# A gated feed-forward kernel on one core: the engines' programs written into the main block, without `nc.Block`

## The chip, the cores and the metric

The kernel runs on one core of one Trainium2 chip. The metric is the device time of one execution in microseconds. Every execution also has a *span*, from the first to the last recorded instruction of the kernel's own program. The time is a little longer than the span (272.68 against 270.87 us in the profiled run of the kernel before). Every profiled run has its span in the trace to the nanosecond; of all other executions the span is recorded to 0.1 us only, so a single "time minus span" of theirs can be off by 0.05 us. Landings and last records are read from the trace's records, which are finer than the views printed here.

## The reference

```python
# B, S, D, F = 32, 32, 1024, 3584; all bfloat16
def reference(x, w_gate, w_up, w_down):
    return (gelu_tanh(x @ w_gate) * (x @ w_up)) @ w_down
```

## The kernel before

The kernel records all operations of all five engines in a list, works out the semaphore waits between them, and then emits each engine's list. It is already tuned: a Strassen-like scheme saves products, and TensorE is busy nearly all the time.

The emission, in which SyncE alone waits at the end for the output transfers:

```python
    def emit(self, e, eng, sems, final=()):
        known = {}
        for op in self.ops[e]:
            ...                                    # waits that are not yet known to be met
            ins = name(eng, *args, **kw) if callable(name) else getattr(eng, name)(*args, **kw)
            if op.wanted:
                ins.then_inc(sems[op.sem], op.step)
        for name, value in final:
            eng.wait_ge(sems[name], value)
```

The block that the emission stands in. Each engine branches into a body of its own and out of it, and all meet at a barrier at the block's end:

```python
        sems, totals = pr.finish(nc, es)
        with nc.Block() as block:
            for name, e in (("sync", "sp"), ("scalar", "act"), ("gpsimd", "pool"), ("tensor", "pe"), ("vector", "dve")):
                getattr(block, name)(lambda eng, e=e: pr.emit(
                    e, eng, sems, [("out", totals["out"])] if e == "sp" else ()))
```

And the head, eight warm-up matmuls on a constant, eight transposes of the first input, then real matmuls as their weights land:

```python
        one = nc.const_aps.tensor(1.0, [P, 512], BF16)
        ...
        for n in [512] * 6 + [P] * 2:
            mm(3, one[:, 0:P], one[:, 0:n], True, True)
        for i, eng in enumerate(("sp", "act")):
            dma(eng, xn[:, 2 * i:2 * i + 2, :], x_r[:, 2 * i:2 * i + 2, 0:NX * P], 0, f"xn{i}")
        ...                                        # weights: q = 0 and 1, on SyncE and ScalarE
        for k in range(NX):
            for i, b in enumerate((6, 7) if k == 0 else (4, 5)):
                half = ps[:, b, 0:P].bitcast(BF16)
                for t in range(2):
                    pr.add("pe", "transpose", half[:, t * P:(t + 1) * P], xn[:, 2 * i + t, k * P:(k + 1) * P], ident[:, :])
                pr.add("dve", "tensor_copy", xT[0][:, k, i * 256:(i + 1) * 256], half)
```

Of the kernel before, what the change touches and what calls it, by code (L numbers as in the profile page):

```python
# [123 lines left out]
def bass_standalone__geglu_ffn__sampling_kernel(  # L124
# [19 lines left out]
    pr = _Program()  # L144

    with ExitStack() as es:
# [469 lines left out]
            dma("sp", out_r[:, 3, c0:c1], o11[:, 3, c0:c1], end, "out")  # L616

        sems, totals = pr.finish(nc, es)
        with nc.Block() as block:
            for name, e in (("sync", "sp"), ("scalar", "act"), ("gpsimd", "pool"), ("tensor", "pe"), ("vector", "dve")):  # L620
                getattr(block, name)(lambda eng, e=e: pr.emit(
                    e, eng, sems, [("out", totals["out"])] if e == "sp" else ()))


# [1 line left out]
_INS = ['x', 'w_gate', 'w_up', 'w_down']  # L626
_OUTS = [((32, 32, 1024), 'bfloat16')]
# [23 lines left out]
```

## Time and profile before

| | before |
|---|---|
| time, median of the first 3 runs | 272.45 us (272.02 to 272.67) |
| profiled run: time, span | 272.68 us, 270.87 us |
| TensorE busy | 267.8 us, 99% of the span |
| first matmul starts | 0.77 us |
| last output landed / last record | 270.459 / 270.867 us |

The profile's page of the kernel before, its head, its busy table and two of its rows by slice (each digit is the busy share, or the granted TensorE clock, of one fortieth of the span, in tenths):

```profile
span 270.9 us, 3344 instructions
PE 267.8 (99%) x1206; PEld 192.5 (71%) x1206; DVE 208.1 (77%) x246; ACT 136.1 (50%) x221; POOL 37.1 (14%) x23
PE   8999999999999999999999999999999999999996
PEclk9999999999999999999999999999999999999999
```

TensorE bounds the kernel; what a change of the program's frame can win lies in the first slice, the last one, and outside the span.

The chain of waits that ended last, in order of time (start, duration, what):

```profile
0.73 0.04 issue
0.77 3.79 PE ps L117 x16
4.56 0.05 issue
4.61 264.07 PE ps L117 x1190
268.67 0.03 issue
268.70 0.29 DVE o L117
```

The row of 1190 matmuls: all real products, 264.07 us without a gap. After it come one copy and the last output's transfer.

Seven of the eleven rows of the block's end in the kernel before (engine's queue, operation, count, duration in ns, first and last start in us; L619 is the `with` line):

```profile
L619 POOLq EVENT_SEMAPHORE  x2: 17/17/17, 270.7 to 270.8; - x2
L619 POOLq DRAIN  x1: 4349/4349/4349, 157.8 to 157.8; - x1
L619 ACTq DRAIN  x1: 519/519/519, 267.9 to 267.9; - x1
L619 DVEq DRAIN  x1: 330/330/330, 268.7 to 268.7; - x1
L619 SPq COMPARE_BRANCH  x1: 37/37/37, 270.5 to 270.5; - x1
L619 SPq DRAIN  x1: 13/13/13, 270.6 to 270.6; - x1
L619 PEldq EVENT_SEMAPHORE  x1: 51/51/51, 270.8 to 270.8; - x1
```

The drains of the other engines end by 269.04 us, while SyncE still waits for the outputs (the last landed at 270.459). Only what starts at 270.5 or later is on the path: SyncE's branch, its drain, GpSimd's two semaphore steps (gather, release) and the engines' last steps. Note that no entry branch, and no exit branch but SyncE's (37 ns), has a record.

### The profile page before, as it was taken

To read this page: it belongs to the slowest core of one execution; us is meant where nothing else is said; L and a number is where in the kernel's file an instruction comes from. 1 tells how busy PE (TensorE), PEld (TensorE's weight loads), DVE (VectorE), ACT (ScalarE), POOL (GpSimd) and SP (SyncE) were. 2 spreads that over 40 slices of the span, in tenths; PEclk is the share of its full clock that TensorE was granted. 3 is DMA by queue.
4 is the path that set the end of the run, shared out by engine and by line. 5 is a ranking of instruction groups with operands and counts; after the bars stand their busy time and mean duration, and the time that the engine had idled before them with its cause. 6 is when DMAs were issued, how large, how long until landed. Compare 5 with 4: busy or idle time off the path is not lost.

```text
span 270.9 us, 3344 instructions
## 1 busy us (share of the span) xinstructions
PE 267.8 (99%) x1206; PEld 192.5 (71%) x1206; DVE 208.1 (77%) x246; ACT 136.1 (50%) x221; POOL 37.1 (14%) x23
## 2 busy tenths in 40 slices
PE   8999999999999999999999999999999999999996
PEld 4444448888888888888776776664458888888884
DVE  1338998998899889988764839289966999999911
ACT  1339876666756675667455564521220305067452
POOL 1000003113311331134345060000000000000000
PEclk9999999999999999999999999999999999999999
DMA  7999850140491002882900070293010000002102
GB/s 211 230 333 224 243 157 4 32 123 0 130 291 46 0 0 80 239 266 73 240 0 0 0 265 8 86 348 112 0 39 19 4 0 0 0 0 80 58 21 97
DMA packets 45024, 27.47 MB, mean 101 GB/s; under 512 B 8656, under 2 KB 45008, under 8 KB 45008
## 3 DMA queue, kind: packets, MB, share of 16 engines
q1 hardware_dynamic: 42496, 25.04, 32.9%
q10 hardware_dynamic: 2512, 2.23, 3.3%
q8 instruction: 9, 0.15, 0.3%
q14 instruction: 7, 0.06, 0.1%
HBM read 23.33 MB, written 2.10 MB: 94 GB/s over the span
## 4 chain that ended last, share of the span: by engine, by line
PE 99%; DVE 0%; issue 0%
PE ps L117 99%; DVE o L117 0%
## 5 line engine op out<-in xcount | busy, mean ns | idle before, releaser
L117 PE MATMUL ps<-S,T 128*128 128x512 f32 x560 | 129.2, 392 | 0.0
L117 PEld LDWEIGHTS ps<-S,T 128*128 128x128 f32 x560 | 105.2, 188 | 22.3
L117 ACT ACTIVATE tmp<-ps 128x512 f32<-128x512 f32 x64 | 38.0, 595 | 51.7 <-PE ps L117 51.5
L117 POOL TENSOR_TENSOR T<-arena 128x1024 fp32r<-128x1024 bf16 x17 | 36.4, 2153 | 124.2 <-PE ps L117 81.8
L117 PE MATMUL ps<-T,S 128*128 128x512 f32 x224 | 51.3, 390 | 0.0
L117 DVE TENSOR_TENSOR T<-arena,T 128x1024 fp32r<-128x1024 bf16 x42 | 51.0, 1220 | 0.2
L117 PEld LDWEIGHTS ps<-T,S 128*128 128x128 f32 x224 | 42.1, 188 | 8.8
L117 ACT ACTIVATE ps<-ps 128x512 f32<-128x512 f32 x44 | 25.6, 584 | 37.0 <-PE ps L117 37.0
L117 DVE TENSOR_TENSOR hT<-tmp,ps 128x512 bf16<-128x512 f32 x56 | 36.9, 684 | 8.7 <-PE ps L117 6.7
L117 PE MATMUL ps<-arena 128*128 128x512 bf16 x192 | 43.2, 384 | 0.0
L117 DVE TENSOR_TENSOR tmp<-ps,tmp 128x512 f32<-128x512 f32 x28 | 19.4, 692 | 23.6 <-PE ps L117 23.6
L117 PEld LDWEIGHTS ps<-arena 128*128 128x128 bf16 x192 | 18.4, 99 | 23.4 <-issue 1.8
L117 DVE TENSOR_TENSOR T<-arena 128x1024 fp32r<-128x1024 bf16 x25 | 30.0, 1221 | 4.3 <-PE ps L117 4.3
L117 DVE TENSOR_TENSOR ps<-ps,tmp 128x512 f32<-128x512 f32 x32 | 22.3, 695 | 3.0 <-PE ps L117 3.0
L117 PE MATMUL ps<-arena,hT 128*128 128x512 bf16 (+2 forms) x126 | 24.6, 356 | 0.0
L117 PEld LDWEIGHTS ps<-arena,hT 128*128 128x128 bf16 x126 | 11.6, 98 | 12.8 <-issue 0.5
L117 ACT ACTIVATE tmp<-tmp 128x512 f32<-128x512 f32 x28 | 17.6, 631 | 2.4 <-DVE tmp L117 2.1
L117 ACT ACTIVATE ps<-hT 128x512 f32<-128x512 f32 x22 | 13.0, 599 | 7.6 <-DVE hT L117 7.6
L117 DVE TENSOR_TENSOR S<-hT 128x1024 fp32r<-128x1024 bf16 x14 | 16.6, 1221 | 0.0
L117 ACT ACTIVATE T<-arena 128x1024 fp32r<-128x1024 bf16 x14 | 14.8, 1060 | 0.0
L117 PE MATMUL ps<-S 128*128 128x512 f32 x56 | 12.9, 389 | 0.0
L117 ACT ACTIVATE hT<-ps 128x512 f32<-128x512 f32 x18 | 9.5, 602 | 6.1 <-PE ps L117 6.0
(33 smaller groups left out, 94.3 us busy)
## 6 DMA issues: line engine op xcount, KB each, us to landing
arena<-in_w_down_dram SPq DMA_DIRECT2D x4, 1792.0 KB, 9.7
arena<-in_w_gate_dram SPq DMA_DIRECT2D x10, 512.0 KB, 5.2
arena<-in_w_up_dram SPq DMA_DIRECT2D x10, 512.0 KB, 6.0
out_dram<-arena SPq DMA_DIRECT2D x12, 128.0 KB, 1.7
arena<-in_w_up_dram ACTq DMA_DIRECT2D x6, 128.0 KB, 4.6
arena<-in_w_gate_dram SPq DMA_DIRECT2D x3, 256.0 KB, 5.3
arena<-in_w_up_dram SPq DMA_DIRECT2D x3, 256.0 KB, 5.5
arena<-in_w_gate_dram SPq DMA_DIRECT2D x4, 128.0 KB, 3.9
```

The costliest lines, as they stand in the source:

```text
L117: ins = name(eng, *args, **kw) if callable(name) else getattr(eng, name)(*args, **kw)
```

## The change

It is meant to take away the branches into and out of the bodies and the barrier of all engines at the end. Nothing else depends on the barrier: SyncE waits for the output transfers anyway, and these wait for everything.

```diff
-        with nc.Block() as block:
-            for name, e in (("sync", "sp"), ("scalar", "act"), ("gpsimd", "pool"), ("tensor", "pe"), ("vector", "dve")):
-                getattr(block, name)(lambda eng, e=e: pr.emit(
-                    e, eng, sems, [("out", totals["out"])] if e == "sp" else ()))
+        for e, eng in (("sp", nc.sync), ("act", nc.scalar), ("pool", nc.gpsimd), ("pe", nc.tensor), ("dve", nc.vector)):
+            pr.emit(e, eng, sems, [("out", totals["out"])] if e == "sp" else ())
```

## The prediction

> **What bounds the kernel now.** TensorE. The page's busy table has PE busy 267.8 of 270.9 us (99%), the chain of work that ended last is 99% PE, and the granted clock is 1.000. The first matmul starts at 0.77 us; the chain's last piece, a VectorE copy, ends at 268.99. So the head is some 0.75 us and the tail some 2 us. The timed number, 272.45, is about 1.8 us longer than the span (the profiled run: 272.68 against 270.87).
>
> **What the change removes.** The built programs differ only in this: one branch per engine into its body, one out of it, and at the end a drain and a semaphore step on every engine (two steps on GpSimd). Order, matmuls, transfers and all other waits are identical. The barrier at the *start*, after GpSimd's constant fills, is not the block's and stays. SyncE's wait for the output transfers stays too: it rode on SyncE's exit branch and becomes a semaphore instruction.
>
> **Costs, from the trace's records.**
> - Entry: the start barrier is released at 0.61 us, the engines' semaphore steps are at 0.65 to 0.67, the first DMA issues at 0.73 to 0.74. SyncE has 68 ns from the end of its step to its first issue, and no entry branch has a record. GpSimd's two neighbouring semaphore steps are 62 ns apart with no branch between, so the branch can hardly be worth more than some 30 ns.[...]
> - Exit of the other engines: their drains end by 269.04, off the path; SyncE waits for the outputs until 270.48.
> - End: SyncE's branch 270.476, its drain 270.646, GpSimd's gather 270.684 and release 270.762, the engines' last steps 270.804 to 270.867. In their place comes one semaphore step of SyncE (17 ns in this trace), ending about 270.50. That removes 0.37 us after the last transfer, all of it on the path.
>
> **Sum.** Span: 270.87 - 0.37 - (0 to 0.03), about 270.5 us. The timed number should fall by the same, with a chance of a little more[...]. Predicted 272.05 us, 0.15% below 272.45: less than the spread of the three runs before (272.02 to 272.67), so the verdict should be "same".
>
> **What would show it.** Right: the last record is SyncE's wait at about 270.5, with no drain or barrier after it; first issues within 0.05 us of where they were; PE busy 267.8; time minus span near 1.8 us. Wrong at the entry: a first matmul over 0.1 us earlier. Wrong at the end: a tail not shorter by 0.3 us, or time minus span growing by what the span loses: the launch's own end absorbed it.
>
> **What would make it wrong.** A chip that runs some tenths of a us elsewhere;[...] the removed barrier having hidden work that the launch does anyway at the end.
>
> Range 271.5 to 272.5 us; faster by over 2%: 0.01, within 2%: 0.98, slower: 0.01.

The sum came to 272.45 - 0.37 - 0.03 = 272.05 us, with the end at 0.37, the entry branches at their most and the "little more" at nil.

## The result, and the profile after

| | before | after |
|---|---|---|
| median (range), 6 runs each | 272.29 us (272.02 to 273.01) | 272.25 us (271.68 to 272.38) |
| ratio, 95% interval | | 0.999 (0.9973 to 1.0007) |
| profiled run: time, span | 272.68, 270.87 us | 272.38, 270.84 us |
| last output landed / last record | 270.459 / 270.867 us | 270.810 / 270.844 us |
| time minus span, profiled run | 1.81 us | 1.54 us |
| time minus span, spans recorded to 0.1 us | 1.78 us (that run; the others have no span on record) | 1.51 to 1.58 us (six runs) |

A ratio here is the mean time of one kernel's runs over that of the other's runs of the same rounds, so it is not quite the ratio of the medians quoted.

The two traces say something more than "too small to see". The page's head and busy table after:

```profile
span 270.8 us, 3333 instructions
PE 268.2 (99%) x1206; PEld 192.6 (71%) x1206; DVE 208.2 (77%) x246; ACT 136.1 (50%) x221; POOL 37.1 (14%) x23
```

The chain of waits that ended last, after:

```profile
0.73 0.04 issue
0.77 3.79 PE ps L117 x16
4.56 0.05 issue
4.61 264.41 PE ps L117 x1190
269.02 0.02 issue
269.04 0.29 DVE o L117
```

And all that is left at the end of the program, SyncE's wait (L121 is the line of the final wait):

```profile
L121 SPq EVENT_SEMAPHORE  x1: 17/17/17, 270.8 to 270.8; - x1
```

So the tail did shrink as intended: from the last output's landing to the last record it was 0.408 us and is 0.034. But the same 1190 matmuls took 264.41 instead of 264.07 us. The gain of 0.374 us was given back almost whole by 0.34 us *inside* TensorE's work, which the change did not touch.

Laying the two traces' matmuls side by side shows where: all but 0.04 us of it arises at one place, the 20th and 21st matmul. TensorE's weight loads there, before and then after (start, duration, engine, what, count; each stands just ahead of its matmul):

```profile
5.41 0.15 PEld L117 LDWEIGHTS ps<-arena 128*128 128x128 bf16 x1 [0.28 <-issue]
5.84 0.15 PEld L117 LDWEIGHTS ps<-arena 128*128 128x128 bf16 x1 [0.28 <-issue]
6.14 0.96 PEld L117 LDWEIGHTS ps<-arena 128*128 128x128 bf16 x5 [0.15 <-issue]
```

```profile
5.42 0.15 PEld L117 LDWEIGHTS ps<-arena 128*128 128x128 bf16 x1 [0.28 <-issue]
5.84 0.15 PEld L117 LDWEIGHTS ps<-arena 128*128 128x128 bf16 x1 [0.28 <-issue]
6.27 0.15 PEld L117 LDWEIGHTS ps<-arena 128*128 128x128 bf16 x1 [0.28 <-issue]
6.67 0.53 PEld L117 LDWEIGHTS ps<-arena 128*128 128x128 bf16 x3 [0.25 <-issue]
```

Nobody waits for data (the first weights, which these matmuls use, had landed by 4.6 us, when the first real matmul started). The matmuls are 427 ns apart and then, from one moment on, 216 ns: TensorE's rate doubles. A matmul that is half through at that moment has an odd length, which tells the moment: before it lies at 6.01 us (a matmul of 300 ns from 5.84 on; and the trace's clock record begins there), after at about 6.64 us (a matmul of 400 ns from 6.27 on: 373 ns at half rate and the rest at full). From 4.61 us to the doubling every real matmul costs twice its time, so by this estimate (6.01 - 4.61) / 2 = 0.70 us are lost before and (6.64 - 4.61) / 2 = 1.01 us after; the difference is 0.31 us.

Two traces don't tell what sets the moment of the doubling. If it differs from execution to execution of one and the same program, the 0.31 us are chance; if it doesn't, they might belong to the changed program.

### The profile page after: what moved, and what is told of

Read it like the earlier page. It is cut to its first block, busy times and chain, and to the rows that moved or that the text cites. A ratio compares the mean times of both kernels' runs of the same rounds, so it can differ in the third digit from the quotient of the medians.

```text
span 270.8 us, 3333 instructions
## 1 busy us (share of the span) xinstructions
PE 268.2 (99%) x1206; PEld 192.6 (71%) x1206; DVE 208.2 (77%) x246; ACT 136.1 (50%) x221; POOL 37.1 (14%) x23
## 3 DMA queue, kind: packets, MB, share of 16 engines
q10 hardware_dynamic: 2512, 2.23, 3.3%
## 4 chain that ended last, share of the span: by engine, by line
PE 99%; DVE 0%; issue 0%
PE ps L117 99%; DVE o L117 0%
```

## The experiments

Three theories. A: the moment of doubling is chance, another in each execution of either kernel. B: it belongs to the program, so that the change gives its own gain back. C: what the program's end loses, the launch's own end (outside the span) takes up again. The following runs told them apart.

### Both kernels once more, unchanged

No edit; the two files again, five timed rounds each on one chip.

> The kernel before once more, unchanged, to see what differs from execution to execution. In the first pair of traces the tail after the last output landed was 0.408 us before and 0.034 after, but TensorE ended 0.345 us later after, all of it arising at its 20th and 21st matmul, where the matmuls go from 427 ns apart to 216 ns: at 6.01 us before, at about 6.64 after (from a matmul that took 400 ns). Theory A (the moment at which TensorE's rate doubles is chance, another one in each execution, of either kernel): this copy's rate doubles at a moment other than 6.01[...], and its spans spread by 0.5 us or more, with time minus span steady at about 1.8 us. Theory B (the moment belongs to the program: without branches the rate doubles later, which gives the gain back): 6.0 us again within 0.1, and spans within 0.2 us of 270.9. Theory C (the launch's own end takes up what the program's end loses) says nothing of this run.

> The changed kernel once more. Its six runs so far had spans of 270.1 to 270.8 and a time minus span of 1.51 to 1.58 us, against 1.78 in the one profiled run of before. Theory A: the rate doubles at a moment other than 6.64 us, spans spread as before_again's do; the last record comes 0.03 to 0.04 us after the last output landed, so span minus the doubling's share is 0.37 us shorter than before_again's; the mean time is 0.35 to 0.65 us below before's, with a standard error of 0.2. Theory B: 6.6 us again, spans near 270.8. Theory C: time minus span grows by 0.37 us against before_again's, to about 2.1.

(The first of these two texts also gave a range for A's moment of doubling. It rested on no trace or run of this case and is cut.)

Measured: `before_again` 271.98 to 272.95 us (median 272.15) and spans of 270.2 to 271.2, a spread of 1.0 us between executions of one and the same program; its rate doubled at 3.45 us. That falsifies B's 6.0 within 0.1. It also lies below the range that A's text had named: A was right that the moment would be another, not in where it would lie. `after_again` had a median of 271.87 us (271.38 to 272.44), ratio to before 0.998 (0.9964 to 0.9996), spans of 269.9 to 270.9; its rate doubled at 6.62 us. Taken by itself, this second 6.6 is what B expected and not what A did, so the two copies don't settle A against B yet; the later traces do.

The chain of waits in `before_again` shows what happens when the doubling comes early, at 3.45 us:

```profile
1.76 4.81 DMA arena<-in_w_gate_dram
6.57 0.05 issue
6.61 261.68 PE ps L117 x1182
```

Now the head is bound by the second weight transfer, which landed at 6.57 us: TensorE's idle time just before its matmul at 6.61 us was 0.30 us in this trace. An early doubling is worth less than it would be if the weights were there.

### A head that hides the doubling, first try

VectorE does a memset (0.92 us) and seven adds of 1.22 us for which the transposes wait, and TensorE gets 24 long warm-up matmuls. In both kernels alike:

```diff
-        for n in [512] * 6 + [P] * 2:
+        for n in [512] * 24 + [P] * 2:
             mm(3, one[:, 0:P], one[:, 0:n], True, True)
+        pr.add("dve", "memset", hT[:, 0:2, :], 0.0)
+        for _ in range(7):
+            gate = tt(S[:, 0:2, :], hT[:, 0, :]..., hT[:, 1, :]..., ADD, 0)
...
-  pr.add("pe", "transpose", ..., ident[:, :])
+  pr.add("pe", "transpose", ..., ident[:, :], after=[gate])
```

> The kernel before with a head that hides the doubling: 24 instead of 6 of the 512-column warm-up matmuls[...] and, on VectorE, seven 128x1024 adds of 1.22 us (about 9.5 us in all) for which the first transposes wait. So all real matmuls run at the full rate and start at the same time in each execution. Expected by all theories: some 4.5 to 5.5 us slower than before. Theory A: spans of the runs within 0.15 us of each other, where those of before spread by 0.5 and more. Theory B: no smaller spread than before's.

> The changed kernel with the same head, to be compared with before_quiet alone. Theory A: span shorter than before_quiet's by 0.37 us (0.34 to 0.42), time shorter by 0.37 to 0.65, every run of it below every run of before_quiet. Theory B: with the doubling hidden the loss is gone as well, so the same 0.37 us shorter; B is told from A by the two copies, not here. Theory C: span 0.37 us shorter but the time within 0.1 us of before_quiet's.

(The time that the 24 warm-up matmuls would take: the 427 and 216 ns give 5.2 to 10.2 us.)

This failed. `before_quiet` took 279.19 to 280.85 us, `after_quiet` 278.53 to 279.91. The adds ended at about 10.8 us, later than estimated, and TensorE sat idle for 2.7 us in the trace of `before_quiet`:

```profile
10.80 0.62 PE L117 MATMUL ps<-ident,hT 128*128 128x128 bf16 x8 [2.69 <-DVE S L117]
```

(The 2.9 us of the next text reckon from the last warm-up matmul's start and its 56 ns, not from its modelled end.) The stretches of `before_quiet` (us, busy time of PE, PEld, DVE, ACT and POOL with counts, granted clock, DMA share, GB/s):

```profile
10.00:11.30 1.30, 0.49 (x8) 0.45 (x8) 0.92 (x2) 0.00 (x0) 0.00 (x0) 1.00 1.31 220
11.40:14.70 3.30, 2.96 (x8) 1.02 (x8) 0.61 (x4) 0.00 (x0) 0.00 (x0) 0.50 0.44 88
14.80:20.00 5.20, 5.20 (x26) 2.34 (x25) 2.48 (x4) 2.06 (x4) 0.00 (x0) 1.00 0.41 116
```

The granted clock was halved again, from 11.35 to 14.77 us. So after 2.69 us without a matmul and eight transposes from 10.80 us on, the rate was lost; whether other matmuls in the place of the transposes would have kept it, no run here shows. Four of the five executions of `before_quiet` and three of the five of `after_quiet` have a mean clock of 0.994 and are 1.2 to 1.7 us longer than the others: the intervention made the noise that it was meant to take away. Only the executions with a mean clock of 1.0 could be compared: 279.19 us against 278.54 and 278.53.

### The same head with 31 warm-up matmuls

The edit is `[512] * 31` in place of `[512] * 24`, so that TensorE idles less before the gate opens.

> The first quiet head failed: TensorE idled 2.9 us before the gate opened at 10.87 us, and the clock record shows the rate halved again from 11.35 to 14.77 us. Now 31 instead of 24 warm-up matmuls of 512 columns: they end at some 9.5 to 11.0 us (worked out from 427 and 216 ns), so at most some 1.4 us of idling. Theory A (the moment of doubling is chance): no second halving, spans within 0.3 us of each other and near the 277.4 of the one run of the first quiet head whose mean clock was 1.0. Theory B (the moment belongs to the program): no prediction apart from the same spread as the kernel before had. Time minus span 1.79 us, as in the 17 runs of before (1.75 to 1.85).

> The changed kernel with that head, to be compared with before_quiet31. Theory A: span 0.37 us shorter (0.3 to 0.45); time minus span 1.54 us as in the 12 runs of after (1.48 to 1.58); time 0.62 us shorter (0.5 to 0.75), every run below every run of before_quiet31. Theory C (the launch's own end takes up the gain): time shorter by 0.1 us or less.

(The 9.5 to 11.0 us are the author's estimate. They come out from the first quiet trace: 10.87 - 2.9 us, and seven more matmuls of 216 to 427 ns each.)

| | before_quiet31 | after_quiet31 | difference |
|---|---|---|---|
| time, mean (range) | 279.22 us (279.18 to 279.26) | 278.60 us (278.55 to 278.63) | -0.62 us |
| span, mean | 277.38 | 277.00 | -0.38 |
| time minus span, mean | 1.84 | 1.60 | -0.24 |
| doubling in the trace | 5.94 us | 3.86 us | |
| last output to last record, in the trace | 0.403 us | 0.034 us | -0.37 |

This is the clean measurement. With the doubling hidden, the executions of one program agree within 0.1 us, every run of the changed kernel lies below every run of the other, and the change is worth 0.62 us, or 0.22%. C is out: the launch's end takes up nothing. On the contrary, a further 0.24 us is won there. On the kernel's own head the executions scatter too much to show the same: there the means of the changed kernel lie 0.28 us (first rounds) and 0.52 us (the second copies) below the kernel before. The real matmuls show how well the head hides the doubling. Chain of waits in `before_quiet31`, then in `after_quiet31`:

```profile
11.77 263.42 PE ps L117 x1190
```

```profile
11.76 263.39 PE ps L117 x1190
```

Doublings two microseconds apart, and the same work within 0.03 us.

### Where the time after the span goes: all engines wait

Over all executions of the unmodified kernels, time minus span was 1.80 us before (42 executions, 1.75 to 1.87) and 1.54 us after (12, 1.48 to 1.58). Here all five engines end with the wait that SyncE alone had, without a barrier:

```diff
-            pr.emit(e, eng, sems, [("out", totals["out"])] if e == "sp" else ())
+            pr.emit(e, eng, sems, [("out", totals["out"])])
```

> The changed kernel, but all five engines, not SyncE alone, end with the wait for the output transfers: no barrier, no branch, yet all engines end at the same late moment. Time minus span fell from 1.79 to 1.54 us with the change. Theory D (the time after the span is shorter because four engines reach the launch's own end early): time minus span back at 1.79, within 0.06. Theory E (it is shorter because less code follows, drains and branches that the launch's end had to wait for): stays at 1.54. Span: the tail after the last output landed grows from 0.03 to at most 0.1 us.

Time minus span went up to 2.19 us (2.14 to 2.23), and the time was 272.18 to 272.79 us. E (less code) is refuted, since there is no drain and no branch in this program. D is right in kind but not in size: letting all engines end late costs 0.65 us, more than the barrier had cost.

### The barrier alone, put back

```diff
             pr.emit(e, eng, sems, [("out", totals["out"])] if e == "sp" else ())
+        nc.all_engine_barrier()
```

> The changed kernel with one barrier of all engines put back at the end, without branches. Theory A: the tail after the last output landed is 0.408 us less what SyncE's branch cost: between its record's end, 270.513, and its drain, 270.646, lie 133 ns[...]; so 0.30 to 0.36 us, which makes the barrier about nine tenths of what the change removes and the branch the rest. If the branches were the main cost, 0.15 us or less. Time minus span by theory D 1.79, by theory E between 1.54 and 1.79.

(The range of 0.30 to 0.36 us rests on the author's estimate of how much of the 133 ns would remain without the branch; no run had shown it.)

Three rows of the barrier, put back:

```profile
L621 POOLq EVENT_SEMAPHORE  x2: 17/17/17, 270.1 to 270.2; - x2
L621 SPq DRAIN  x1: 7/7/7, 270.1 to 270.1; - x1
L621 PEldq EVENT_SEMAPHORE  x1: 51/51/51, 270.3 to 270.3; - x1
```

The tail from the last output to the last record was 0.287 us, time minus span 1.82 us (1.77 to 1.84), the time 272.03 to 272.87 us. Of the 0.374 us by which the tail shrank, 0.287 - 0.034 = 0.253 us belong to the barrier and the other 0.12 us to SyncE's exit branch and its drain's later start. So the barrier is two thirds, not the nine tenths that were expected. The whole change of time minus span comes with the barrier, none with the branches.

### Which engine is late: one engine waits in SyncE's place

The edit gives the final wait to GpSimd, TensorE or ScalarE, and takes it from SyncE:

```diff
-            pr.emit(e, eng, sems, [("out", totals["out"])] if e == "sp" else ())
+            pr.emit(e, eng, sems, [("out", totals["out"])] if e == "pool" else ())     # "pe", "act"
```

> With all five engines waiting at the end, time minus span was 2.19 us (2.14 to 2.23), with SyncE alone 1.54, with a barrier put back 1.82. So each engine seems to have something of its own to do after its last instruction, which runs while SyncE waits when the engine ends early. Here GpSimd alone waits for the outputs in SyncE's place. Theory F (one engine's end work is the long one, and GpSimd, whose drain took 0.19 us at the start against 0.01 on SyncE, is it): time minus span near 2.19. Theory G (all engines' end work is alike, and adds up or queues): between 1.4 and 1.7.

> TensorE alone waits for the outputs, after its last matmul. Theory F with GpSimd as the long one: time minus span near 1.54, as with SyncE. If TensorE is the long one: near 2.19. Theory G: 1.4 to 1.7.

> ScalarE alone waits for the outputs. Theory F with GpSimd as the long one: near 1.54. Theory G: 1.4 to 1.7. If one of the three is clearly below SyncE's 1.54, the final wait belongs there.

| the engine that ends last | time minus span (range) | executions |
|---|---|---|
| SyncE (the changed kernel) | 1.54 us (1.48 to 1.58) | 12 |
| ScalarE | 1.71 us (1.69 to 1.72) | 3 |
| TensorE | 1.78 us (1.76 to 1.81) | 3 |
| GpSimd | 2.20 us (2.18 to 2.22) | 3 |
| all five | 2.19 us (2.14 to 2.23) | 4 |

F holds: GpSimd is the long one, 0.66 us longer than SyncE, and all five together take as long as GpSimd alone. The runs were on several chips, but that is not the cause: with SyncE last, `early_issue5` below, on the chip of the three single-engine runs, had 1.56 us, and `after_quiet31`, on the chip of the all-five run, 1.60. The author's reading of these five rows is that each engine has something to do after its last instruction, side by side with the others, and that GpSimd's is hidden behind the rest of the kernel if its last work is over long before (at some 162 us here). No record shows that work itself. The small expectation that ScalarE and TensorE be like SyncE failed: they are 0.17 and 0.24 us longer. The kernel as changed has its final wait on the best of the four engines tried.

One thing stays open. With the block's barrier, GpSimd ended 0.09 us before the span's end and all the same the time outside was 1.80, not 2.1. It had drained early, at 157.8 to 162.1 us by its record, which may be what saves the rest. The last record behind the barrier is TensorE's, and 1.80 us is close to the 1.78 that TensorE takes alone. No run separates these.

### The doubling in all traces

The moment at which TensorE's rate doubled, read off from the odd-length matmul or the clock record, in the traces whose head is the kernel's own, with the chain's row of 1190 matmuls:

| trace | entry and exit branches | doubling, us | 1190 matmuls, us |
|---|---|---|---|
| before | yes | 6.01 | 264.07 |
| before_again | yes | 3.45 | (stalled by a transfer) |
| after | no | 6.64 | 264.41 |
| after_again | no | 6.62 | 264.33 |
| after_final_pe | no | 6.03 | 264.09 |
| after_final_act | no | 4.77 | 263.40 |
| after_final_pool | no | 4.19 | 263.43 |
| after_barrier | no | 3.98 | 263.43 |

And `after_allwait`, without branches too, doubled at 3.82 us. With the four traces of the hiding heads that is 3.45 to 6.01 us in four traces with branches and 3.82 to 6.78 us in nine without (`early_issue5` below, with another head, has 5.25). The moments are spread over 3.33 us, from 3.45 to 6.78; what sets them, no run here shows. B is out: the changed programs' moments cover the whole range and the two programs that happened to double at 6.01 and 6.03, one with branches and one without, needed 264.07 and 264.09 us for the 1190 matmuls. The row of `after_final_act`, where the doubling came before they began:

```profile
4.80 263.40 PE ps L117 x1190
```

So of the first pair's traces, the one before lost 264.07 - 263.40 = 0.67 us to the half rate and the one after 1.01 us.

### An attempt at a better kernel

The experiments point at the head, so one more program moved the first input transfer of SyncE and of ScalarE ahead of the start barrier, by moving the two instructions in the finished main block ahead of that engine's drain, and took one long warm-up matmul away:

```diff
-        for n in [512] * 6 + [P] * 2:
+        for n in [512] * 5 + [P] * 2:
...
+        block = nc.main_func.blocks[0]
+        todo = list(block.instructions)
+        for eng in (nc.sync, nc.scalar):
+            mine = [i for i in todo if i.engine == eng.engine]
+            drain = next(i for i in mine if type(i).__name__ == "InstDrain")
+            first = next(i for i in mine if type(i).__name__ == "InstDMACopy")
+            todo.remove(first)
+            todo.insert(todo.index(drain), first)
+        block.instructions = todo
```

> Not for the cause but for a better kernel: the changed kernel with the first input transfer of SyncE and of ScalarE issued ahead of the start barrier (it needs nothing that the barrier guards: at 0.0 to 0.15 us instead of 0.73) and, as the first operands land sooner, five instead of six long warm-up matmuls (427 ns each at the half rate). Where the trace's head is bound by transfers (first weights landed at 4.0 to 4.6 us, the second at 5.1 to 6.9) all of it should move some 0.5 us ahead, the issue time of one transfer; where it is bound by TensorE at the half rate, 0.43 us by the missing matmul. Expected: 0.3 to 0.5 us below the changed kernel's mean of 271.99, so about 271.6, and 0.6 to 0.9 below before in the same rounds. If the start is bound by something else (ScalarE arriving at the barrier 0.1 us later, or by the transfers' landing times whatever their issue), within 0.1 us of the changed kernel.

It is not better: 271.59 to 273.73 us, ratio to before 1.0001 (0.9977 to 1.0025). The first operands did land sooner (2.68 and 3.06 us instead of 3.25 and 3.48), but SyncE and ScalarE came to the start barrier late, so that the first matmul moved from 0.77 to 1.01 us. Four of the six executions lie at 271.59 to 272.06 us, two at 273.66 and 273.73 with spans 1.6 us and more above the others. By the estimate used above, which takes half of the time at the half rate as lost, 1.6 us would be a doubling some 3.2 us later; but no trace of such an execution was taken, so this is only argued.

## Why the prediction was right or wrong

- **The number.** 272.05 us was predicted with a range of 271.5 to 272.5; the measured median is 272.25, and over all 12 executions of the changed kernel with its own head the mean is 271.99. The verdict "same" was right.
- **Entry branches worth nothing (0 to 0.03 us).** Right: SyncE's first issue started at 0.739 us before and at 0.737 after, the first matmul at 0.773 and 0.771. What the prediction said on how a branch might stall was not shown; the bound of some 30 ns is its estimate from the 68 and 62 ns of the trace before.
- **The end, 0.37 us off the span.** Right in size and place: 0.374 us in the first pair, 0.369 in the quiet pair. Its parts were not told apart in the prediction; the runs give the barrier about 0.25 and the branch with what follows it about 0.12 us.
- **"A chance of a little more" outside the span.** This is the term that was mis-sized. The sum took it as nil and named "time minus span near 1.8 us" as the sign of being right. It fell to 1.54 us (1.48 to 1.58 in the 12 executions). The runs show that it matters which engines end late: with the barrier put back it is 1.82 us again, and when GpSimd alone is made to end last it is 2.20. So the change is worth 0.62 us where the head is hidden, not 0.4.
- **"The last record is SyncE's wait at about 270.5", PE busy 267.8.** The first is wrong in the profiled run (270.84), and PE was busy 268.2. The missing step is the run-to-run moment of TensorE's doubling. The prediction named the granted clock of 1.000 and no slower stretch; but that mean leaves out the first 6.01 us, before the clock record begins. The matmuls 427 ns apart in the first six microseconds were there to be seen.
- **"Less than the spread of the three runs before."** Right, and the spread now has a place, the head: with it hidden, executions agree within 0.1 us. What differs there from trace to trace is the doubling and, when it comes early, the landing of the first inputs and weights that TensorE then waits for (inputs at 3.73 us in `after_barrier`, weights at 6.57 in `before_again`); how much each adds was not separated.

## What to carry to other kernels

Look at time minus span as well as at the span: here it was 1.54 us with SyncE's single wait for the outputs, 1.82 with a barrier of all engines after it (which took about 0.25 us of the span besides), and 2.20 with the wait on GpSimd. So, where a single wait for the outputs will do, let an engine that has nothing left to do run to its own end. Before you explain some tenths of a microsecond between two traces, find the moment at which TensorE's matmuls fall from 427 to 216 ns apart in each of them, because it differs from execution to execution (3.45 to 6.78 us in these traces); compare stretches after it, or hide it in both kernels with a common head, and check by the granted clock that the head doesn't lose the rate again (as `before_quiet` did after 2.69 us without a matmul). A frame of barriers and branches was worth 0.62 us once per execution here, measured with the doubling hidden (279.22 against 278.60).
